# Loading and folding K's weight in halves of columns, decay vectors first, one output row in two halves: a gated mix of a state-space layer and linear attention

## The chip, the cores and the metric

The kernel runs on one core of a Trainium2 chip. A core has a matrix engine (PE, with its weight loads shown apart as PEld), a vector engine (DVE), a scalar engine (ACT), a general engine (POOL) and a queue engine that issues transfers (SP); ACT and POOL can issue transfers too. The metric is device time in microseconds, from the first to the last thing that the execution does. A profile is one execution with every instruction recorded; its "span" runs from the first to the last instruction, and the execution's own time is a little longer than that.

## The reference

The input x has 2048 rows of 512 values. Two branches read it, and a gate mixes them row by row:

```
g = sigmoid((x * gate_w).sum(-1))
out = g * A(x) + (1 - g) * B(x)
```

A is a diagonal state-space layer: x is projected to 512 complex states, each state runs the recurrence h = Lam_bar * h + Bu over the 2048 rows, with Lam_bar = exp(exp(log_dt) * (Lambda_re + i Lambda_im)), and the states are projected back; x * Dskip is added.

B is linear attention with 32 heads of 16 values. Q, K and V are x times three 512 x 512 blocks of wqkv. Q and K go through a small 16 x 16 matrix per head (w_phi), then through softmax of the result and of its negative, which gives 32 features per head; kv and z are sums over all rows of K's features (with V, and alone); each row's Q features read them, the quotient num / den is the head's output, and a 512 x 512 matrix wo ends the branch. All inputs and the output are bfloat16.

## The kernel before, in words

The rows are handled in 16 tiles of 128. x is loaded transposed, one tile by one DMA transpose from the SP queue (`x_load`, L228), into xT. w_phi is the same for all rows, so it is folded into the weights of Q and K once: a block-diagonal matrix BD is built from w_phi (`st_B`, L343, on DVE, with a mask that comes from an identity matrix made on POOL), K's weight is transposed on PE (`st_W`, L271), multiplied with BD (`fold`, L428, called by `st_f`), and copied to SBUF as Wk2. A K tile is then four matmuls of 512 columns (`st_k`, L477, through `tile_mm`), copied to Xq by `evac` (L117), on ACT or on DVE. Q's weight goes the same way later (`st_w`), V needs no fold (`st_v`).

K's features: DVE takes maxima and minima over the 16 values of a head by trees (`feat_max`, `feat_min`; the lines L511, L521, L527), ACT takes the exponentials (`feat_exp`, L138), DVE sums them (`feat_sum`), ACT takes logarithm and exponential of the sums, DVE scales. PE accumulates K's features with V over all tiles (`st_a`, L578). Q's features are made the same way in four groups of four tiles (A, 1, 2, 3), and are then transposed by DMA from SP (phT, L563).

The state-space branch interleaves rows by 8: input projections (`st_g`, L601, which need BT, the transposed B matrices, loaded as Bn by L284 and transposed by DMA at L288), a scan on DVE (`st_z`), and steps `st_h` that fill in the seven rows between. Its decay factors are small vectors: Lambda_im, Lambda_re and log_dt are loaded from POOL's queue into vec_n (L251, after the identity matrices and an iota), transposed on PE (`st_V`, L310), copied to vec (L312), and then a chain of short instructions on DVE and ACT makes angles, sines and powers (`st_P`, `st_P2` to `st_P4`, `st_U`, `st_i`, `st_M`). ACT holds one table set at a time, Exp/Ln or Sin: L130 loads the first, the first Sin (L144) brings the second, and L130 in `st_L` brings back the first.

Output: for every tile, `st_y` accumulates the state-space part in PSUM, `st_o` makes the attention output and transposes it (by DMA from SP, L758, or on PE for the last four), `st_t` multiplies with wo into the same PSUM bank, scales the row tile by the gate (L769 on ACT or L771 on DVE) and stores it (L773, from SP or ACT).

The order of the work is written out by hand. Every step is a Python generator that yields after each instruction group; the string ORDER names, word by word, which step runs on next. `k0@2` starts step k0 with PSUM bank 2, a later `k0` runs its next group, `:D` puts a copy or a scaling on DVE and not on ACT, `:A` puts a store on ACT's queue and not on SP's, and `F:28` issues 28 matmuls of 128 columns on a constant tile ("spin", results unused). PE, DVE, ACT and SP execute their instructions in just this order; an instruction that waits holds up all behind it on its engine.

Of the kernel before, what the change touches and what calls it, by code (L numbers as in the profile page):

```python
# [23 lines left out]
ORDER = """
B F:28 l11 F:4 W1@0 W0@1 W2@2 W1:D f1@3 W3@4 f1 W0:D f0@5 f0 NR W2:D f2@6 W3:D f3@0 f3 f2:D V@1 V P P P P2 P2 P2 P2 P2
P4 U P3 P4 P4 i1 i2 U l12 i1 i2 U F:4 k0@2 k0 NI P2 P3 l10 i0 l9 k1@3 k1 x0 i1 i1 i0 i2 k3@4 l14 x0 k2@5 n0 U M i1 k2
V2@6 v3@1 i2 x0 i0 v0@7 i0:D i0 v2@0 x0 k3 l8 n0 l13 i3 x0 k5@2 k5 i3 k4@3 v0 R0 x1 k6@5 n0 n0 i3 i3:D x1 x1 i2 k4 n0
v1@4 i3 L V2 k7@2 k7 n1 n1 x1 n1 gw x1 n1 R1 v6@7 e0 e0 v1 k6:D v4@6 n1 x2 n2 v7@3 v7 k11@2 v6 s0 x2 s0 e1 n2 s0 v5@5
v5 s0 s0 R2 D k12@4 R3 k10@3 k9@7 v4 k8@5 n2 l15 s0 e1 k13@6 v2 s1 k10 k14@0 s0 k11 C1 Q2 k8 C4 g20@3 s1 x2 k13 a0@25
k14 a0 n2 s1 k12 g20 x2 g00@6 k9 g30@0 s1 s1 s1 x2 n2 s1 v3 g40@4 x3 g01@3 g10@7 n3 R5 g00 a1 a1 x3 g60@1 n3 e2 R4  # L30
g11@6 g10 x3 g01 n3 e2 x3 e2 e2 n3 g11 k15@3 g60 g10 g30 g40 x3 s2 n3 g70@1 k15 g11 s2 x4 s2 s2 n4 g30 Q1 Q3 x4 n4 e3
e3 x4 C5 n4 Q0 x4 g50@7 g50 g50 s2 g21@4 n4 g21 s2 s2 v8@3 e3 e3 s3 g70 g70 g70 z0 s3 z0 g31@6 g31 s3 z0 z0 v11@0
g41@7 a2 C6 a2 g41 z0 z0 v11 g61@4 a2 g61 C7 w0@1 w0 C3 w1@7 w1 g31 a2 w2@0 w2 w3@4 s3 s3 g51@1 g51 g51 z0 R7 z0 x4
g62@7 w3 z0 z0 g71@6 g71 g02@0 v8 n4 s3 J2 g71 g71 z1 g02 z1 h50@1 h50 J2 z1 e4 e4 q1@4 h10@3 g62 g12@6 h10 g22@0 q2@1
z1 z1 z1 g22 q2 s3 z1 z1 q1 e4 h60@3 h60 g12 g12 z1 q3@7 q0@0 q0 q3 g32@1 e4 xA C2 g42@4 g32 nA g32 s4 g42 v9@6 v9 z1
s4 C0 J0 J0 g52@0 g52 c4 g52 nA c4 xA c4 R6 g72@7 g72 J1 s4 nA g23@3 g43@1 g03@4 g63@6 g72 g72 z2 h51@0 J3 c5 a3 g23
z2 J1 v10@7 h11@3 nA a3 c2 c2 g03 xA z2 z2 z2 z2 c0 h51 h61@4 z2 z2 g13@0 v10 xA h11 g43 c3 g13 a3 a3 J3 c5 z2 s4
g33@7 g13 g33 c0 z2 s4 s4 g33 h32@1 c2 h32 xA g53@3 g63 h52@0 g53 g53 nA s4 h52 h42@7 h42 eA c5 eA v14@1 v14 g73@6 g73
g73 q5@3 g73 h61 h12@0 h12 v12@1 v15@7 z3 z3 c0 z3 v12 eA eA h21@4 z3 v13@6 h21 a4 z3 z3 sA v13 z3 z3 c3 q10@0 q10
q6@1 v15 sA c1 c1 q4@4 q4 q6 a4 a4 c3 a4 h20@6 h30@0 h30 c7 q8@7 q12@4 q8 Y Y sA z3 z3 h33@2 q5 sA sA c1 h62@1 h20  # L40
h02@0 h33 sA sA q7@7 h62 G h43@3 h53@6 h02 c7 h13@2 Y Y sA q7 y6@1 h13 h01@0 h53 q12 c7 sA sA c6 q14@5 q14 h23@7 h23
h22@4 h31@2 h00@6 c6 q13@5 h31 h41@7 h43 c6 h22 h40@3 h63@2 h00 h41 h63 h40 h03@6 h03 sA sA y3@4 y3 END X1 o0@7 N1 X1
q13 o0 o0@2 O o0 N1 X1 q9@6 q9 N1 o1@3 X1 o1 o1@5 q11@7 o0 N1 X1 N1 o3@2 o1 o3 q11 X2 o1 o1 h01 X2 N2 X2 o3@6 o3 N2 X2
N2 E1 E1 E1 o1 E1 o0 o0 X2 S1 S1 N2 y0@3 o2@5 y0 y0 o2 o2@2 y3 o2 o2 y1@7 y1 S1 o3 o3 o3 S1 G y2@0 N2 q15@6 q15 S1 S1
o2 y1 o2 t1 S1 S1 G G y9@5 y9 E2 E2 y4@2 y4 y2 N3 E2 E2 y5@6 y9 y5 t1 S1 S1 S1 S1 X3 t3 t3 y2 t2 t2 X3 N3 N3 S2 X3 S2
t0 o4@7 y5 o4 o4@4 o4 N3 o4 X3 S2 y4 t0 y13@0 S2 o4 o5@7 o5 o5@4 o5 o5 y6 o4 y6 o6@3 S2 o6 o6@7 o6 X3 o5 y7@4 y7 o5 S2
S2 o7@3 N3 y13 o6 t4 t0:A o6 o6 E3 E3 E3 S2 S2 y8@7 t4:D o7:D E3 S3 t5 S2 S2 S2 t5 y12@2 S3 S3 o7@3 o7 o7 o7 t6 t6
o8@6 o8 o8@3 o8 o7 y12 y8 S3 t1:A o8 o8 o9@1 o9 o9@6 o8 y11@3 y11 S3 S3 y10@1 o9 o9 o9 S3 S3 t4:A o11@6 y7 t7 y12 o9
o11 t7 o10@6 y8 t8 t8 y11 y13 o11@4 t9 S3 S3 S3 o10 o11 S3 o10@7 t9:D y15@6 y14@4 o11 o11 o10 o10 t8:A o12@7 o12 o12@5
o12:D y15 o10 o12 o12 o11 o13@7 o13 o13@5 o13 o13 t2 y14 y14 o10 o12@7 t7:A t5:A o12:D o14@5 o14:D t3:A y10 o15@7 t9:A  # L50
y10 o15 o15@5 o15:D o15 o13 t12 o15 o14@7 o14 o14 t12:D t12 t11 t11:D o15@5 o15 o13@7 t10 t6:A t11 y15 o13:D t10 t10
t15 t15 t15:A o14 o14@2 t13 o14:D t13 t13 t14 t14 t14:A
# [16 lines left out]
def kernel(  # L69
# [198 lines left out]
    live = {}  # L268
    MM = nc.tensor.matmul

    def st_W(j):  # L271
        pt = bank([P, KT, P], BF16, "ptw")
        for k in range(KT):
            nc.tensor.transpose(pt[:, k, :], wk_nat[:, j, k * P:(k + 1) * P], ident[:])
# [198 lines left out]
    def tile_mm(pt, ti, W):  # L473
        for kt in range(KT):
            MM(out=pt[:], lhsT=xT[:, kt, ti * P:(ti + 1) * P], rhs=W[:, kt, :], start=(kt == 0), stop=(kt == KT - 1))  # L475
# [285 lines left out]
    def st_t(n):  # L761
        ti = order[n]
        py, oT = live["py", n], live["oT", n]
        for g in range(HG):
            MM(out=py[:], lhsT=oT[:, g, :], rhs=Wo[:, g, :], start=False, stop=(g == HG - 1))  # L765
        yield
        ot = pools["op"][1].tile([P, D], BF16, name="ot", bufs=14)
        if sel["eng"] == "act":
            nc.scalar.mul(out=ot[:], in_=py[:], mul=G[:, ti:ti + 1])  # L769
# [78 lines left out]
```

## Time and profile before

| | |
|---|---|
| median of 3 runs | 157.01 us (156.79 to 157.65) |
| the profiled execution's own time | 156.63 us |
| its span | 154.6 us |
| PE busy | 147.7 us, 96% |
| DVE busy | 131.8 us, 85% |
| ACT busy | 129.4 us, 84% |
| POOL busy | 16.1 us, 10% |
| granted PE clock, mean | 1.000 |

Busy time of PE counts the whole of each matmul, whose ends overlap with the next one's start, so 96% busy does not say that it runs at its peak; starts of matmuls have to be read for that. For DVE and ACT, too, one instruction's end overlaps with the next one's start by some 0.1 us. "Idle before, releaser" names what ended an engine's wait. SP, and the queues of ACT and POOL, show only the issue of a transfer as an instruction; the landing is later and is given as "to landing" from the start of the issue.

### The profile page before, as it was taken

The numbers are of one execution on the slowest core, as the hardware profiler recorded it, in microseconds if no ns is written. First come the engines' busy times: TensorE is split into PE (matmuls) and PEld (weight loads), VectorE is DVE, ScalarE is ACT, GpSimd is POOL, SyncE is SP. The second block draws the span as 40 slices with busy tenths as digits, with TensorE's granted clock in tenths as the row PEclk, the third lists the DMA queues.
The fourth block names the chain that finished last, engine by engine and source line by source line (L and its number), as shares of the span: only waits on it lengthen the run. The fifth ranks groups of instructions, "written<-read, shape, count | busy, mean of one in ns | idle before, by whom it ended". The sixth has DMA issues, their size and how long they took to land.

```text
span 154.6 us, 3382 instructions
## 1 busy us (share of the span) xinstructions
PE 147.7 (96%) x1254; PEld 95.6 (62%) x1254; DVE 131.8 (85%) x303; ACT 129.4 (84%) x279; POOL 16.1 (10%) x43
## 2 busy tenths in 40 slices
PE   7999999999999999999999999999998999989990
PEld 7844444797789876888755767454454545545540
DVE  3789999999999999999999999999997966423730
ACT  3489999999999999999999996799497998465652
POOL 8239980000000000000000000000000000000000
PEclk9999999999999999999999999999999999999999
DMA  4785998465475849910000006943169689789742
GB/s 120 158 222 87 168 191 170 89 98 107 97 78 105 174 94 168 184 25 6 0 0 4 0 0 136 141 136 68 34 123 143 117 163 197 150 137 200 208 147 94
DMA packets 50848, 17.55 MB, mean 113 GB/s; under 512 B 44176, under 2 KB 50832, under 8 KB 50832
## 3 DMA queue, kind: packets, MB, share of 16 engines
q1 hardware_dynamic: 48544, 15.36, 53.2%
q10 hardware_dynamic: 2128, 1.97, 4.5%
q8 instruction: 10, 0.16, 0.4%
q14 instruction: 6, 0.05, 0.1%
q0 software_dynamic: 160, 0.01, 0.1%
HBM read 2.64 MB, written 2.10 MB: 31 GB/s over the span
## 4 chain that ended last, share of the span: by engine, by line
DVE 47%; PE 32%; DMA 8%; ACT 6%; issue 4%; DVEq 0%; SPq 0%
PE py L717 9%; DVE smk L511 6%; PE pk L475 6%; DMA oT<-on 5%; PE py L765 5%; PE pgq L601 4%; DMA phT<-EEq 3%; DVE Bn L672 3%; DVE EEk L548 3%; DVE w L641 3%; DVE HM L672 3%; DVE H L652 3%; PE spin L812 3%; DVE EEk L527 2%; DVE EEk L521 2%
## 5 line engine op out<-in xcount | busy, mean ns | idle before, releaser
L601 PE MATMUL pgq<-xT,BT 128*128 128x256 bf16 x256 | 31.2, 272 | 0.0
L475 PEld LDWEIGHTS <-xT 128*128 128x128 bf16 x192 | 18.3, 98 | 18.6 <-DMA xT<-in_A_x_dram 0.8
L601 PEld LDWEIGHTS <-BT 128*128 128x128 bf16 x256 | 24.7, 98 | 3.9
L138 ACT ACTIVATE EEk<-EEk 128x1024 bf16<-128x1024 bf16 x20 | 20.6, 1075 | 0.3 <-DVE EEk L527 0.3
L765 PE MATMUL py<-Wo,oT 128*128 128x512 bf16 x64 | 16.1, 379 | 0.9 <-DMA oT<-on 0.9
L119 ACT CAST uv<-pgq 128x512 bf16<-128x512 f32 x28 | 16.3, 604 | 0.3
L475 PE MATMUL pq<-Wq,xT 128*128 128x512 bf16 x64 | 15.8, 379 | 0.0
L475 PE MATMUL pv<-Wv,xT 128*128 128x512 bf16 x64 | 15.6, 379 | 0.0
L475 PE MATMUL pk<-Wk,xT 128*128 128x512 bf16 x64 | 15.0, 379 | 0.3 <-ACT EEk L138 0.3
L138 ACT ACTIVATE ld<-pn 128x16 f32<-128x16 f32 x32 | 6.2, 193 | 7.6 <-PE pn L736 7.4
L138 ACT ACTIVATE EEq<-EEq 128x1024 bf16<-128x1024 bf16 x12 | 11.8, 1061 | 0.3 <-DVE EEq L527 0.3
L590 ACT ACTIVATE phT<-X,dgB 128x512 bf16<-128x512 bf16 x16 | 11.5, 740 | 0.0
L769 ACT ACTIVATE ot<-py,G 128x512 bf16<-128x512 f32 x12 | 8.0, 684 | 3.5 <-PE py L765 3.3
L119 ACT CAST nu<-pn 128x256 bf16<-128x256 f32 x28 | 10.3, 381 | 0.0
L736 PEld LDWEIGHTS <-phT 128*128 128x128 bf16 x128 | 6.7, 98 | 5.3 <-DMA phT<-EEq 1.2
L765 PEld LDWEIGHTS <-oT 128*128 128x128 bf16 x64 | 5.6, 97 | 6.2 <-DMA oT<-on 1.2
L119 ACT CAST vx<-pv 128x512 bf16<-128x512 f32 x16 | 9.4, 600 | 0.0
L548 DVE TENSOR_TENSOR EEk<-EEk,rck 128x4096 bf16<-128x4096 bf16 (+1 forms) x5 | 9.3, 1859 | 0.0
L119 ACT CAST Xq<-pq 128x512 bf16<-128x512 f32 x16 | 9.1, 610 | 0.2
L736 PE MATMUL pn<-KVm,phT 128*128 128x68 bf16 x128 | 8.0, 194 | 0.8 <-DMA phT<-EEq 0.7
L119 ACT CAST Xq<-pk 128x512 bf16<-128x512 f32 x15 | 8.4, 618 | 0.4 <-PE pk L475 0.4
L511 DVE TENSOR_TENSOR smk<-smk 128x512 bf16<-128x512 bf16 (+4 forms) x18 | 8.6, 476 | 0.1
(177 smaller groups left out, 319.6 us busy)
## 6 DMA issues: line engine op xcount, KB each, us to landing
X<-HM SPq DMA_DIRECT2D x8, 256.0 KB, 4.0
out_dram<-ot ACTq DMA_DIRECT2D x11, 128.0 KB, 2.5
out_dram<-ot SPq DMA_DIRECT2D x5, 128.0 KB, 2.5
C2r<-in_B_wqkv_dram ACTq DMA_DIRECT2D x2, 256.0 KB, 3.3
Wv<-in_B_wqkv_dram SPq DMA_DIRECT2D x1, 512.0 KB, 4.0
Bn<-in_A_B_re_dram SPq DMA_DIRECT2D x1, 512.0 KB, 5.5
Bn<-in_A_B_im_dram SPq DMA_DIRECT2D x1, 512.0 KB, 6.7
Wo<-in_B_wo_dram SPq DMA_DIRECT2D x1, 512.0 KB, 4.6
```

The costliest lines, as they stand in the source:

```text
L119: nc.scalar.copy(out=out_ap, in_=in_ap)
L138: ins = nc.scalar.activation(**kw)
L475: MM(out=pt[:], lhsT=xT[:, kt, ti * P:(ti + 1) * P], rhs=W[:, kt, :], start=(kt == 0), stop=(kt == KT - 1))
L511: VT(out=dst, in0=cur[:, :, :, 0:n, :], in1=cur[:, :, :, n:2 * n, :], op=op)
L548: VT(out=E5, in0=E5, in1=rc.to_broadcast([P, L, 2 * NB, Dh, 4]), op=ALU.mult)
L590: nc.scalar.mul(out=t_, in_=x_, mul=c_)
L601: MM(out=pg[:, h, :], lhsT=BT[:, kt, 2 * j + h, :], rhs=xT[:, kt, r * NC:(r + 1) * NC], start=(h == 0 and kt == 0), stop=(r % 2 == 0 and k ...
L672: VT(out=dst, in0=ph[:], in1=uv[j][:, r], op=ALU.add)
L717: MM(out=py[:], lhsT=hs(r, t, slice(a * P, (a + 1) * P)), rhs=C2B[t], start=(t == 0), stop=False)
L736: MM(out=pn[:, 4 * m:4 * m + 4, :].rearrange("p h e -> p (h e)"), lhsT=ph[:, 4 * hf + m, :], rhs=KVm[:, 4 * hf + m, :], start=(m == 0), st ...
L765: MM(out=py[:], lhsT=oT[:, g, :], rhs=Wo[:, g, :], start=False, stop=(g == HG - 1))
L769: nc.scalar.mul(out=ot[:], in_=py[:], mul=G[:, ti:ti + 1])
```

## The change

- K's weight comes from memory in two halves of columns (each with all 512 rows, 256 columns, so runs of 512 bytes), and not in two halves of rows (runs of 1024 bytes). The transposes of `st_W` then take a column block each and write one contiguous block of WTk; two of the four copies stand on ACT (W1, W3), two on DVE (W0, W2), where all four stood on DVE.
- The four fold steps make a half of the columns for two row blocks each, so the first two (f0, f1) need only the first half of the weight. The first four K tiles are computed in two halves of columns, eight matmuls of 256 columns each; their copy to Xq stays whole.
- The three loads of vec_n move ahead of the identity matrices on POOL's queue. The two loads of vec_m stay after the iota.
- Step t15 scales its row tile in two halves of columns and stores the halves with two transfers, one from ACT's queue, one from SP's. It is the last tile by number; t13 and t14 still come after it in the order, whole.
- ORDER is written anew. The multiset of steps is the same but for the extra groups of k0 to k3 and t15, and the constant matmuls: 24 and 4, where 28, 4 and 4 stood. The second part of B's input matrix (NI, A_B_im) is now the first of the two loads of Bn and stands ahead of the eight later x tiles on SP; the other one (NR) stands behind four of them (tiles 11, 14, 13, 8) and ahead of tiles 12, 9 and 10; tile 15's load stands after two of the BT transposes. Engine changes beside W1 and W3: the copy of f1 on DVE and that of f2 on ACT (before: the other way round), k7 for k6 on DVE, the absolute value of i3 on ACT (before on DVE), the scalings of t5 and t7 on DVE and those of t9, t11 and t12 on ACT, a copy of o13 on ACT and one more of o15 on DVE. The order of nearly all else shifts by some places.

```
-B F:28 l11 F:4 W1@0 W0@1 W2@2 W1:D f1@3 W3@4 f1 W0:D f0@5 f0 NR W2:D f2@6 W3:D f3@0 f3 f2:D V@1 V P P P P2 P2 P2 P2 P2
-P4 U P3 P4 P4 i1 i2 U l12 i1 i2 U F:4 k0@2 k0 NI P2 P3 l10 i0 l9 k1@3 k1 x0 i1 i1 i0 i2 k3@4 l14 x0 k2@5 n0 U M i1 k2
...
+NI B F:24 W1@0 W0@1 W1 W3@2 W3 W0:D V@3 V W2@4 W2:D P f0@5 f0 P f1@6 P F:4 l11 f1:D f3@0 P2 f2@1 k1@3 U f3 P2 f2 P2
+P2 P4 k0@2 P4 P4 P2 V2@4 k2@7 k0 k0 P3 P3 l14 k3@5 k1 k2 i0 i2 V2 i0 k1 k3 U i1 l13 k2 i2 i1 i1 U n0 i0 x0 i2 i0:D l8
+v3@6 v0@0 i0 k4@1 n0 NR n0 x0 l12 i2 v3 n0 l9 k5@4 x0 x0 i3 v4@2 l10 R0 k6@3 i3 k7@7 i2 x0 R1 i1 v2@6 n0 k3 x1 n1 i1
...
+T_SPLIT = (15,)
+K_SPLIT = 4
...
-    for k0 in (0, 2):
-        nc.scalar.dma_start(out=wk_nat[:, k0:k0 + 2, :], in_=B_wqkv[k0 * P:(k0 + 2) * P, D:2 * D].rearrange("(k p) n -> p k n", p=P))
+    for t_, srcs in ((vec_n, (A_Lambda_im, A_Lambda_re, A_log_dt)),):
+        for n, src in enumerate(srcs):
+            nc.gpsimd.dma_start(out=t_[4 * n:4 * n + 4, :], in_=src.rearrange("(j p) -> j p", p=P))
+    HD = D // 2
+    for c in range(2):
+        nc.scalar.dma_start(out=wk_nat[:, :, c * HD:(c + 1) * HD],
+                            in_=B_wqkv[:, D + c * HD:D + (c + 1) * HD].rearrange("(k p) n -> p k n", p=P))
...
-    def st_W(j):
+    def st_W(k):
         pt = bank([P, KT, P], BF16, "ptw")
-        for k in range(KT):
-            nc.tensor.transpose(pt[:, k, :], wk_nat[:, j, k * P:(k + 1) * P], ident[:])
-        yield
-        evac(WTk[:, :, j * P:(j + 1) * P], pt[:])
+        for j in range(KT):
+            nc.tensor.transpose(pt[:, j, :], wk_nat[:, j, k * P:(k + 1) * P], ident[:])
+        yield
+        evac(WTk[:, k, :].rearrange("p (j d) -> p j d", j=KT), pt[:])
         yield
...
-    def st_f(d):
-        return fold(Wk2, WTk, d)
+    def st_f(n):
+        c, d0 = n // 2, n % 2 * 2
+        pf = bank([P, 2, HD], F32, "pf")
+        for k in range(2):
+            for d in range(2):
+                MM(out=pf[:, d, k * P:(k + 1) * P], lhsT=WTk[:, 2 * c + k, (d0 + d) * P:(d0 + d + 1) * P], rhs=BD[:, 2 * c + k, :], start=True, stop=True)
+        yield
+        evac(Wk2[:, d0:d0 + 2, c * HD:(c + 1) * HD].rearrange("p d (hh f hl) -> p d hh f hl", hh=4, f=Dh),
+             pf[:].rearrange("p d (hh hl f) -> p d hh f hl", hh=4, hl=4))
+        yield
...
-        tile_mm(pk, ti, Wk2)
-        yield
+        if ti < K_SPLIT:
+            for c in range(2):
+                for kt in range(KT):
+                    MM(out=pk[:, c * HD:(c + 1) * HD], lhsT=xT[:, kt, ti * P:(ti + 1) * P], rhs=Wk2[:, kt, c * HD:(c + 1) * HD],
+                       start=(c == 0 and kt == 0), stop=(kt == KT - 1), skip_group_check=True)
+                yield
+        else:
+            tile_mm(pk, ti, Wk2)
+            yield
...
+        if n in T_SPLIT:
+            cols = [slice(c * D // 2, (c + 1) * D // 2) for c in range(2)]
...
+            for c in cols:
+                if sel["eng"] == "act":
+                    nc.scalar.mul(out=ot[:, c], in_=py[:, c], mul=G[:, ti:ti + 1])
+                else:
+                    VS(out=ot[:, c], in0=py[:, c], scalar1=G[:, ti:ti + 1], scalar2=None, op0=ALU.mult)
+                yield
+            for c in cols:
+                sel["q"].dma_start(out=out_par[:, ti // 2, ti % 2, c], in_=ot[:, c])
+                yield
+            return
```

More of the change, by code (lines that the diff above doesn't have):

```diff
@@ L30 @@
[L30 to L49, printed above, removed]
@@ L50 @@
-o12:D y15 o10 o12 o12 o11 o13@7 o13 o13@5 o13 o13 t2 y14 y14 o10 o12@7 t7:A t5:A o12:D o14@5 o14:D t3:A y10 o15@7 t9:A
-y10 o15 o15@5 o15:D o15 o13 t12 o15 o14@7 o14 o14 t12:D t12 t11 t11:D o15@5 o15 o13@7 t10 t6:A t11 y15 o13:D t10 t10
-t15 t15 t15:A o14 o14@2 t13 o14:D t13 t13 t14 t14 t14:A
+NI B F:24 W1@0 W0@1 W1 W3@2 W3 W0:D V@3 V W2@4 W2:D P f0@5 f0 P f1@6 P F:4 l11 f1:D f3@0 P2 P2 f2@1 k1@3 U f3 P2 f2 P2
+P2 P4 k0@2 P4 P4 P2 V2@4 k2@7 k0 k0 P3 P3 l14 k3@5 k1 k2 i0 i2 V2 i0 k1 k3 U i1 l13 k2 i2 i1 i1 U n0 i0 x0 i2 i0:D l8
@@ new lines @@
+v3@6 v0@0 i0 k4@1 n0 NR n0 x0 l12 i2 v3 n0 l9 k5@4 x0 x0 i3 v4@2 l10 R0 k6@3 i3 k7@7 i2 x0 R1 i1 v2@6 n0 k3 x1 n1 i1
+x1 n1 x1 x1 k4 l15 R2 gw U i3 i3 v1@5 n1 n1 v7@1 x1 k7:D k5 n1 k6 x2 i3 n2 L e0 k11@4 x2 n2 R3 x2 e0 k11 v2 v0 s0 e1
+s0 s0 Q2 s0 s0 k14@3 k14 s0 k13@7 k13 e1 C2 M D s0 v1 s1 v6@4 n2 x2 Q1 v5@6 k12@0 s1 k12 k9@3 k9 k8@7 k8 k10@5 n2 v6
+v5 a0@03 a0 v4 s1 g20@7 x2 k10 C0 v7 s1 g20 s1 g40@4 g40 Q3 g00@6 n2 x3 s1 e2 e2 e2 k15@2 k15 g01@5 g01 g50@1 s1 a1 x3
+a1 g21@7 n3 g00 x3 e2 n3 n3 x3 n3 g60@4 g60 g10@2 g10 g21 x3 C4 C5 g30@5 n3 s2 s2 x4 g10 s2 x4 s2 e3 e3 g11@6 g11 R5
@@ new lines @@
+t4 y12@1 N3 o6 t0:A S2 E3 o6 o6 o7 o7@7 E3 t5 S2 S2 S2 S2 o7:D y8@7 t6 E3 y13 t5:D t4:D E3 S3 o7 t6 S2 o8@2 o8 o8@0 o8
+o8 y13 o7 y11@3 o7 S3 o9@2 o9 S3 o9@0 S3 t4:A o8 S3 S3 o9 y12 y12 y10@2 o8 o9 S3 t1:A o9 o9 t6:A S3 S3 S3 y8 y11 y11
+o11@0 o11 t7 t7:D S3 S3 o11@0 o11 o11 y8 t8 o10@0 t8 t8:A t9 o10 o10@5 t9 o10 o10 o11 y15@7 y14@0 o11 o12@4 o12 o12@5
+y15 o12:D o12 o12 o10 o10 t2:A o13@4 o13 o13@5 o13 t5:A o13 y14 y15 t3:A o14@4 o14 o12@5 o12:D y10 y10 o15@5 t9 o15:D
+o13 o15@4 o15 o15 t12 t12 o14@5 o15 o14:D o14 o14 t11 t11 t12 o13@4 t11 o13 t7:A o15@5 t10 t10 o14@1 o15:D t15 t15 t15
@@ L53 @@
+y14 t10 t15:A t15 t13 t13 t13 o14:D t14 t14 t14:A
 """
 H_VECTOR = tuple((r, j) for r in (1, 2, 4, 5, 6) for j in range(4))
+T_SPLIT = (15,)
+K_SPLIT = 4
 OT_PE = (12, 13, 14, 15)
@@ L248 @@
     nc.gpsimd.iota(iot[:], pattern=[[1, NC]], base=0, channel_multiplier=0, allow_small_or_imprecise_dtypes=True)
-    for t_, srcs in ((vec_n, (A_Lambda_im, A_Lambda_re, A_log_dt)), (vec_m, (A_Dskip, gate_w))):
-        for n, src in enumerate(srcs):
-            nc.gpsimd.dma_start(out=t_[4 * n:4 * n + 4, :], in_=src.rearrange("(j p) -> j p", p=P))
+    for n, src in enumerate((A_Dskip, gate_w)):
+        nc.gpsimd.dma_start(out=vec_m[4 * n:4 * n + 4, :], in_=src.rearrange("(j p) -> j p", p=P))
     M2 = stg.tile([P, 4], F32, name="M2", bufs=1)
@@ L763, in st_t @@
         py, oT = live["py", n], live["oT", n]
+        if n in T_SPLIT:
+            cols = [slice(c * D // 2, (c + 1) * D // 2) for c in range(2)]
+            for g in range(HG):
+                MM(out=py[:], lhsT=oT[:, g, :], rhs=Wo[:, g, :], start=False, stop=(g == HG - 1))
+            yield
+            ot = pools["op"][1].tile([P, D], BF16, name="ot", bufs=14)
+            for c in cols:
[8 more added lines that the diff above has]
+            return
         for g in range(HG):
```

18 lines of the change are left out of this document (15 added, 3 removed).

## The prediction

> **What bounds the kernel now.** I read the page's first part and its chain, then the busy time by stretch, then the order of time at both ends.
>
> ```profile
> span 154.6 us, 3382 instructions
> PE 147.7 (96%) x1254; PEld 95.6 (62%) x1254; DVE 131.8 (85%) x303; ACT 129.4 (84%) x279; POOL 16.1 (10%) x43
> DVE 47%; PE 32%; DMA 8%; ACT 6%; issue 4%; DVEq 0%; SPq 0%
> ```
>
> ```profile
> 10.00:20.00 10.00, 10.00 (x49) 4.43 (x47) 9.90 (x37) 9.77 (x22) 8.66 (x22) 1.00 0.82 146
> 80.00:90.00 10.00, 10.00 (x98) 6.18 (x97) 9.91 (x26) 9.83 (x18) 0.00 (x0) 1.00 0.01 2
> 130.00:140.00 10.00, 9.43 (x85) 5.36 (x84) 3.36 (x6) 5.32 (x20) 0.00 (x0) 1.00 0.87 157
> ```
>
> In each stretch (columns PE, PEld, DVE, ACT, POOL, clock, DMA, GB/s) up to 90 us PE, DVE and ACT are full together. From the starts of matmuls PE also runs at its rate: 512 columns every 0.216 us. Between its first real work (4.4) and its last start the larger gaps are 0.23 and 0.24 (fold steps), 0.48 (23.0), 0.28 (100.2), 0.90 (116.8), 0.74 (136.3) and 0.48 (146.4); from 24 to 100 there is none above 0.05. DVE, taking each kind's usual distance from start to start, idles 0.9 us in all from 8 to 118. So neither engine alone can be made to gain: the end moves if all three start sooner, or if work leaves DVE and a PE gap closes.
>
> ```profile
> 1.11 3.59 PE L812 MATMUL spin<-fillw 128*128 128x128 bf16 x32 [1.11 <-DVE fillw L157]
> 4.50 1.08 PE L274 MATMUL ptw<-ident,C2r 128*128 128x128 bf16 x12
> 7.46 3.62 PE L475 MATMUL pk<-Wk,xT 128*128 128x512 bf16 x16
> 7.95 0.17 DVE L337 TENSOR_TENSOR ssm_par<-vec,ssm_par 128x8 f32<-128x8 f32 x1 [0.43 <-ACT ssm_par L138]
> 9.13 1.28 ACT L144 ACT_TABLE_LOAD   x1
> 16.53 0.59 SPq L284 DMA_DIRECT2D Bn<-in_A_B_im_dram  x1
> 17.48 1.28 ACT L130 ACT_TABLE_LOAD   x1
> 19.25 2.01 ACT L138 ACTIVATE EEk<-EEk 128x1024 bf16<-128x1024 bf16 x2
> 21.29 0.69 DVE L511 TENSOR_TENSOR smk<-EEk 128x1024 bf16<-128x1024 bf16 x1
> 23.69 2.27 PEld L475 LDWEIGHTS <-xT 128*128 128x128 bf16 x12 [0.80 <-DMA xT<-in_A_x_dram]
> ```
>
> The front, in order of time: constant matmuls until the weight is there, K from 7.46, the decay chain on DVE from 7.95, Sin tables at 9.13, Exp tables at 17.48, the first exponentials, the first sum right behind them (21.29), and one wait of PE for an x tile.
>
> ```profile
> 113.06 4.83 DMA phT<-EEq
> 117.94 0.30 PE pn L736 x4
> ...
> 132.98 4.04 DMA oT<-on
> ...
> 151.04 0.69 ACT ot L769
> ```
>
> The chain's end: DVE's last product of query group 1 (111.77) releases a DMA transpose, PE waits 0.90 for it, later 0.74 for an oT; then PE, one scaling, one store.
>
> **The change part by part.** Sums are against the profiled execution, 156.63 (span 154.6 and 2.0 around it); the median is 0.38 above it.
>
> *Weight in column halves, fold, split K.* The first half lands 3.28 after its issue at 0.79 (4.07), the second at 4.67. Packets of 1024 bytes took 46 ns, those of 256 bytes 18; at 512 bytes I estimate 27 from these, so a half's 512 packets over 16 engines need 0.87 instead of 0.74: landing 4.2 and 4.9. The 24 constant matmuls end at 1.11 + 24 x 0.107 = 3.68. So transposes run from 4.25 (before 4.39), 0.43 a step. ACT copies W1 at 4.95, W3 at 5.6, in its idle time (its first copy was at 6.09, after 2.91 idle); DVE copies W0 until 5.77; f0 at 5.83, its copy 6.27 to 6.86; f1's copy on DVE ends at 7.2. K's first half starts at 6.95, its third matmul at 7.25 with 0.22 of work done: as if from 7.03, so **PE leads by 0.43**. [...]
>
> *Decay vectors first on POOL.* Their issues (0.78, 0.53, 0.52) push the identities from 1.46 and 1.70 to 3.3 and 3.5. The transposes need the first at 4.25: covered by 0.9. DVE's mask, two small steps and BD follow at 3.7 to 5.4 (BD before: 3.92 to 4.61), just ahead of the W0 copy; if that slips, f0 does, bounded by 0.7, the shift of BD; I take 0. log_dt lands at 2.10 + 3.20 = 5.3 (before 6.47), V stands behind three transposes, and the decay chain starts on DVE at 6.35, not 7.95: **1.6 sooner**. Of that 0.6 goes to f1's copy, which now stands inside the chain, 0.1 to V2's; vec_m (4.9 + 3.1 = 7.5) is there when PE reaches V2 (7.9).
>
> *ACT.* Last fold copy at 7.95, so the Sin tables load at 7.95 instead of 9.13. Between the two loads stand all four first K copies (before three, one lay ahead), one more later K copy (0.48) and one more absolute value (0.31): the second load comes at about 17.1, the first exponentials at 18.4, not 19.25, since one K copy that stood between is now ahead. The first sum on DVE follows at 20.45: **0.85 sooner**, at equal work done on DVE (19.5 us in both orders). The x trees wait for K copies at 10.5 and 14.3; there DVE would be idle 0.1 to 0.7, and this is why 1.6 becomes 0.85.
>
> *Engine moves.* W1, W3 (0.34 each) and i3's absolute value (0.2) leave DVE: up to the last product of query group 1 it has 0.7 less work in all, some of it already in the 0.85. ACT has 1.1 more, 0.96 of it in early idle time.
>
> *SP and Bn.* NI moves up to 12.5, NR to 18.5 (behind four x tiles at 1.31 each); its landing is not known there: 4.0 (Wv, same size, 6.6 to 10.5) to 6.7 (NI before), nearest 5.5 (NR before, one x tile ahead of it, as here), so 24.0. Tile 12 is issued behind it; tiles behind a Bn load landed 0.44 and 0.58 after it: 24.5 (22.9 to 25.7). PE gets to k12 at 7.03 + 16.5 + 0.18 (the V2 gap) = 23.7, and waits 0.8 where it waited 0.48: there its lead shrinks from 0.43 to about 0.1 (from +0.9 to -1.1 between the ends). R0 needs both Bn loads: 24.1, as before 24.21. Tile 15 is issued at 26.7, lands by 31.3 (4.6), k15 is due at 31: 0 to 0.4.
>
> *Middle and end.* PE is 0.1 to 0.5 ahead, DVE and ACT 0.85; where DVE waits for PE it loses some of it, but its order puts z0 to S1 0.4 to 0.9 us of work earlier than before, so I let 0.85 stand at group 1's last product. Then phT lands at 117.0, where PE arrives at 116.9: the 0.90 gap closes. After that PE's order has the same steps at the same work (t9 at 128.7 us of work in both), and I keep the gaps at 136 and 146.
>
> *t15.* Two scalings for 0.69: from 0.69 (proportional) to 1.38 (no saving); nearest is the cast of 256 columns, 0.37 against 0.60 for 512, so about 0.85. ACT idles 0.42 before t13 and 0.16 before t14, which wait for PE; at worst t14 starts 0.1 later. One more SP issue (0.34) ends before t13's at 150.9. So 0; t14's full scaling and store still end the kernel. t9, t11, t12 against t5, t7: one more 0.69 on ACT, in its 5.0 us idle from 130 to 140: 0.
>
> **Sum:** 156.63 - 0.85 = 155.8, **156.1** against the median.
>
> **The rivals.** (1) *Eaten by the wait for x.* PE leads by only 0.1 at 28 us; if DVE's order then waits for PE wherever it is ahead (x4 behind the accumulation, the h sums at 88 to 96), only PE's lead is left: 156.9. For it: no PE gap from 24 to 100 that could close. Against it: the 0.90 gap belongs to DVE's chain.
>
> (2) *Slower: NR lands 6.7 after its issue.* Then 25.2, tile 12 at 25.7, k12 starts 2.0 late and PE is 1.1 behind before; R0 goes at 25.2 and g20 waits until 28.9. PE has no gap to make it up, DVE waits with it: +1.0, 158.0. It decides from a landing of tile 12 at 24.6 on. For it: NI took 6.68 when x tiles stood ahead of it; against it: NR took 5.54, and Wv 3.95.
>
> (3) *The matrix engine stays at half its rate.* Matmuls of 128 columns start 0.107 apart until 5.0 us, then 0.056. Now PE idles from 3.68 to 4.25, and if the full rate came a stretch like the first (3.9 us) later, the fold's 16 matmuls and K's first would take double: about 0.8 on PE by 8.4, partly hidden by the wait for tile 12: +0.4, 157.4. [...] No row here shows a gap that early.
>
> **How the numbers follow.** Forecast 0.42, own range 155.3 to 156.7; rival 1 0.28; rival 2 0.18; rival 3 0.12. A measurement of this kernel tells about 0.5%, 0.8 us, from no change: faster is below 156.2, slower above 157.8. Forecast gives 0.35 faster, 0.07 same; rival 1 0.04 faster, 0.22 same, 0.02 slower; rival 2 0.16 slower, 0.02 same; rival 3 0.02 faster, 0.05 same, 0.05 slower. Faster 0.41, same 0.36, slower 0.23. The range runs from the forecast's 155.3 to rival 2's 158.1.
>
> **What would show it.** Right: K's first matmul near 7.0, the decay chain near 6.4, Sin tables near 8.0, first exponentials near 18.4, no wait before o4 near 117. Wrong: starts 0.107 apart after 5.0 us; PE waiting over 0.9 for an x tile near 24, or for BT at 28; new PE gaps behind ACT's copies between 40 and 100, where the uv copies left it 0.14 to 0.4; a gap longer than 0.74 before t9.

## The result and the profile after

| | before | after |
|---|---|---|
| median of the executions | 156.82 us (20, from 156.09 to 158.1) | 158.26 us (20, from 156.84 to 159.9) |
| ratio to before, 95% interval | | 1.0065 (1.0036 to 1.0094) |
| profiled execution, its span | 156.63, 154.6 | 157.03, 155.2 |

The change makes the kernel slower by 0.65%, where 0.6% faster was forecast (156.1 us, range 155.3 to 158.1). The executions of the changed kernel fall apart into two groups: of the 15 that the ratio rests on, 6 took 156.84 to 157.34 and 9 took 157.76 to 158.77. The other five, 159.24 to 159.90, are classed as slow and left out of it; the medians in the table, which have them, differ by 0.9%. The profiled execution is of the lower group, so its trace shows only a part of the loss.

The profile page of the changed kernel, first part and chain, and two of its stretches (columns: PE, PEld, DVE, ACT, POOL, granted clock, DMA share, GB/s):

```profile
span 155.2 us, 3400 instructions
PE 147.2 (95%) x1262; PEld 96.6 (62%) x1262; DVE 131.4 (85%) x299; ACT 131.7 (85%) x284; POOL 14.0 (9%) x43
...
DVE 62%; PE 23%; DMA 6%; issue 4%; ACT 2%; POOL 1%; DVEq 0%; SPq 0%; POOLq 0%
```

```profile
10.00:20.00 10.00, 10.00 (x61) 5.72 (x61) 9.60 (x34) 9.75 (x23) 7.03 (x22) 1.00 1.11 167
80.00:90.00 10.00, 10.00 (x100) 6.32 (x99) 9.86 (x24) 9.89 (x18) 0.00 (x0) 1.00 0.01 2
130.00:140.00 10.00, 10.00 (x86) 5.54 (x85) 5.30 (x11) 5.45 (x22) 0.00 (x0) 1.00 1.11 181
```

The middle is as full as before. The differences are at both ends. PE's order of time at the front of the changed kernel (start, length, what; in brackets the idle time before it and what ended it):

```profile
4.08 1.52 PE L280 MATMUL ptw<-ident,C2r 128*128 128x128 bf16 x12 [0.23 <-DMA C2r<-in_B_wqkv_dram]
6.67 0.16 PE L316 MATMUL pvt<-ident,vec_n 12*128 12x12 bf16 x1 [1.07 <-DMA vec_n<-in_A_log_dt_dram]
6.77 0.40 PE L280 MATMUL ptw<-ident,C2r 128*128 128x128 bf16 x4
7.00 0.61 PE L447 MATMUL pf<-BD,Xq 128*128 128x128 bf16 x8
...
8.14 0.74 PE L496 MATMUL pk<-Wk,xT 128*128 128x256 bf16 x5
9.93 0.49 PE L496 MATMUL pk<-Wk,xT 128*128 128x256 bf16 x3 [1.05 <-ACT Wk L121]
```

V, the transpose of the decay vectors, now stands ahead of W2 and of all folds on PE and waits 1.07 us for log_dt. K's first half starts at 8.14 (before, K's first: 7.46), and behind five of its matmuls PE waits another 1.05 for a copy on ACT. The order of time of ACT, and of DVE where the first sum stands, gives the other half of that second wait, and what it does further on:

```profile
8.81 1.07 ACT L121 CAST Wk<-pf 128x512 bf16<-128x512 f32 x2 [0.69 <-PE pk L496]
9.90 1.28 ACT L146 ACT_TABLE_LOAD   x1
...
19.66 1.28 ACT L132 ACT_TABLE_LOAD   x1
20.95 2.00 ACT L140 ACTIVATE EEk<-EEk 128x1024 bf16<-128x1024 bf16 x2
```

```profile
23.05 0.68 DVE L532 TENSOR_TENSOR smk<-EEk 128x1024 bf16<-128x1024 bf16 x1
```

ACT's copies of the second half of the folded weight wait for PE's reads of the first half, though the two share no data. (Below, this is called the false wait.) So the Sin table comes at 9.90 (before 9.13; each of ACT's table loads takes 1.28), the first exponentials at 20.95 (19.25), the first sum at 23.05 (21.29). Late in the kernel the chain runs through the first transpose of query group 1:

```profile
113.07 1.19 DVE EEq L580
114.31 4.97 DMA phT<-EEq
```

DVE is 1.25 us later there (issue 114.31, before 113.06), 0.5 of the 1.76 having been made good. In both traces matmuls of 512 columns start 0.216 us apart where PE does not wait. How much later than at this rate PE's matmuls start, summed over a stretch: 5.03 us in the first ten (before 2.67), 0.13 from 20 to 30 (before 0.74; the wait of 0.48 for tile 12 is gone), 0.70 from 100 to 110 (0.36), 1.70 from 110 to 150 (2.75). Over the whole kernel this makes +1.1 us; eight constant matmuls fewer, at 0.054 by the same rate, take off 0.4; the span is 0.6 longer.

### The profile page after: what moved, and what is told of

Its sections match the earlier page's. It is cut to its first block, busy times and chain, and to the rows that moved or that the text cites. A ratio compares the mean times of both kernels' runs of the same rounds, so it can differ in the third digit from the quotient of the medians.

```text
span 155.2 us, 3400 instructions
## 1 busy us (share of the span) xinstructions
PE 147.2 (95%) x1262; PEld 96.6 (62%) x1262; DVE 131.4 (85%) x299; ACT 131.7 (85%) x284; POOL 14.0 (9%) x43
## 4 chain that ended last, share of the span: by engine, by line
DVE 62%; PE 23%; DMA 6%; issue 4%; ACT 2%; POOL 1%; DVEq 0%; SPq 0%; POOLq 0%
PE py L738 9%; DVE smk L532 8%; PE py L802 6%; DVE EEk L569 6%; DVE mxk L532 5%; DVE mnk L532 5%; DVE EEk L542 4%; DMA phT<-EEq 3%; DVE HM L693 3%; DVE Bn L693 3%; DVE H L673 3%; DMA vec_n<-in_A_log_dt_dram 3%; DVE w L662 2%; DVE EEk L548 2%; PE pn L757 2%
## 5 line engine op out<-in xcount | busy, mean ns | idle before, releaser
L622 PE MATMUL pgq<-xT,BT 128*128 128x256 bf16 x256 | 31.7, 272 | 0.0
L489 PEld LDWEIGHTS <-xT 128*128 128x128 bf16 x176 | 17.0, 98 | 16.4
L140 ACT ACTIVATE EEk<-EEk 128x1024 bf16<-128x1024 bf16 x20 | 21.1, 1106 | 0.0
L802 PE MATMUL py<-Wo,oT 128*128 128x512 bf16 x60 | 14.9, 379 | 0.0
L489 PE MATMUL pk<-Wk,xT 128*128 128x512 bf16 x48 | 11.2, 379 | 0.0
L121 ACT CAST Xq<-pq 128x512 bf16<-128x512 f32 x16 | 9.6, 625 | 1.1 <-PE pq L489 0.9
L532 DVE TENSOR_TENSOR smk<-smk 128x512 bf16<-128x512 bf16 (+4 forms) x18 | 8.1, 449 | 0.2
```

The costliest lines, as they stand in the source:

```text
L140: ins = nc.scalar.activation(**kw)
L532: VT(out=dst, in0=cur[:, :, :, 0:n, :], in1=cur[:, :, :, n:2 * n, :], op=op)
L622: MM(out=pg[:, h, :], lhsT=BT[:, kt, 2 * j + h, :], rhs=xT[:, kt, r * NC:(r + 1) * NC], start=(h == 0 and kt == 0), stop=(r % 2 == 0 and k ...
```

## Experiments

The first theory, A: the loss is made by the two stalls at the front. Its rivals: B, the front has slack and ACT's added work or the new order further on costs; C, the matrix engine's rate or the landing of Bn. Ratios are to the kernel before, run on the same chip beside each group of kernels.

### Undoing the two stalls, and the early vectors

Halves of Wk2 one behind the other (the later K tiles, not split, read both halves through a rearranged view):

```
+    Wk2h = Wk2[:].rearrange("p k d -> p (k d)").rearrange("p (c k n) -> p c k n", c=2, k=KT)
-        evac(Wk2[:, d0:d0 + 2, c * HD:(c + 1) * HD].rearrange(...
+        evac(Wk2h[:, c, d0:d0 + 2, :].rearrange(...
-                    ... rhs=Wk2[:, kt, c * HD:(c + 1) * HD],
+                    ... rhs=Wk2h[:, c, kt, :],
```

> Wk2 is laid out with its two column halves one behind the other (each half's 4 x 256 values contiguous), nothing else changed. Theory A (the loss is made at the front, by two stalls of PE; the second, 1.22 us at 8.6, is a wait between halves that share no data but lie interleaved in one tile): the copy of f3 on ACT no longer waits for k1's first half (8.81 becomes about 8.1), k0's first half follows k1's without the 1.05 wait, the Sin table load goes from 9.90 to about 8.9, the first sum from 23.05 to about 22.1, and the time falls to 0.998 to 1.002 of before (changed kernel: 1.0065). Rival B (PE's front has slack; what costs is ACT's 1.1 us of added work, or the new order further on): the wait goes, the time stays at 1.005 to 1.008. Rival C (the matrix engine's rate or the landing of Bn sets it): as B, and 0.107 between starts after 5 us, or a wait before k12 that takes the gain.

V behind f1:

```
-... W0:D V@3 V W2@4 W2:D P f0@5 f0 P f1@6 P F:4 l11 f1:D ...
+... W0:D W2@4 W2:D f0@5 f0 f1@6 V@3 V P P P F:4 l11 f1:D ...
```

> The transpose of vec_n (V) moves on PE from ahead of W2, f0 and f1 to behind f1's matmuls, its copy on DVE behind W2's; nothing else changed. Theory A: the 1.07 wait for vec_n's landing (6.67) is then filled with W2, f0 and f1; f0 goes from 7.00 to about 6.1, k1's first half from 8.14 to about 7.6; the second stall stays and swallows part of it, so the time is 1.001 to 1.005 of before. Rival B: 1.005 to 1.008. A third reading (the chain of decay vectors, not K, carries the delay): DVE's first product of the chain stays at 7.5 and the first sum within 0.2 of 23.05, time 1.005 to 1.008 too.

Both at once:

> Both of the above: the halves contiguous, and V behind f1. Theory A: both stalls gone, K's first half at about 7.5 and no wait over 0.5 behind it, first exponentials at about 19.3 (before 19.25, changed 20.95), time 0.993 to 0.999 of before. Rival B: 1.005 to 1.008. Rival C: the wait for tile 12 near 24 us comes back with 0.5 to 1.0 and the time stays above 1.000.

The loop that loads vec_n, moved back to just ahead of vec_m's:

> The three loads of vec_n go back behind the identity matrices and the iota on POOL's queue, as in the kernel before; all else as changed. The prediction's step was that moving them first makes the decay vectors land 1.2 sooner. In the changed kernel log_dt landed at 6.54 (before 6.47), so the theory now says: they land at 6.3 to 6.7 here as well, the identities are there by 2.0 and not by 4.1, the first stall stays, time 1.004 to 1.008 of before. If the move did gain something that the one profile does not show, log_dt lands at 7 or later here and the time is over 1.010.

| | median, us | ratio (95%) | V on PE | K's first | first sum |
|---|---|---|---|---|---|
| contiguous halves | 158.31 | 1.0084 (1.0060 to 1.0107) | 6.76 | 9.39 | 24.63 |
| V behind f1 | 156.62 | 0.9989 (0.9966 to 1.0012) | 6.73 | 7.50 | 22.84 |
| both | 157.46 | 1.0023 (0.9999 to 1.0046) | 7.92 | 9.29 | 23.66 |
| vectors back | 161.54 | 1.0226 (1.0174 to 1.0279) | 7.06 | 9.69 | 27.17 |

Theory A explains neither. V behind f1 brought K's first to 7.50 as expected, and the time even below the 1.001 to 1.005 that A had said. But its first sum is only 0.21 earlier than the changed kernel's (22.84 against 23.05), and DVE keeps about this lead up to 120 us; there it grows to 0.65, where a block of PE's code came at 115.09 and not at 117.34 (see the part on PE's code). Most of the rest of the way from 1.0065 to 0.9989 is that the changed kernel's times stand mostly in its upper group; its lower one, near 157.0, would give 1.001. So by these profiles V's own price is about 0.2 us. With the halves the theory failed outright (0.998 to 1.002 expected). The contiguous layout did remove the false wait: ACT's copies now wait for the fold and not for K. (Order of time of ACT, contiguous halves.)

```profile
9.21 1.07 ACT L121 CAST Wk<-pf 128x512 bf16<-128x512 f32 x2 [0.59 <-PE pf L448]
10.30 1.28 ACT L146 ACT_TABLE_LOAD   x1
```

But everything was later, and the reason stands in PE's own rate: with contiguous halves, with both, and with the vectors back, matmuls of 128 columns still started 0.107 us apart at 7 us, and the rate doubled only at 12.9, 9.8, and past 16 us; in the changed kernel's own profile it doubled (to 0.056 apart, below called the full rate) by 5.2, with V behind f1 by 4.5. With the vectors back in their old place log_dt lands at 6.93, not 6.54. Whether the early place is worth these 0.4 us is not shown, since in the kernel before, with the same place and the same issue times, it landed at 6.47. And 0.4 us is not that kernel's 1.6%, for it also has the low rate longest.

### The rate

A new theory, D: in the upper group the full rate comes late, because PE now idles for 0.49 (3.5 us), 0.35 (4.8) and 1.23 (5.4), in the time in which the rate doubles in the lower group. Filling the stretches with constant matmuls starts nothing sooner:

```
-NI B F:24 W1@0 W0@1 W1 W3@2 W3 W0:D V@3 V ...
+NI B F:27 W1@0 W0@1 W1 F:4 W3@2 W3 W0:D F:11 V@3 V ...
```

> The changed kernel with constant matmuls put into the idle stretches of PE's front and nothing else: 27 in place of 24 ahead of W1, 4 ahead of W3, 11 ahead of V. Theory D (new, from the runs before: the matrix engine's rate decides; in three of the four kernels it stood at 0.107 between starts of 128 columns until 9.8, 12.9 and past 16 us, and the changed kernel's own executions fall into a group near 157.0 and one from 157.8 to 159.9): with no gap over 0.2 ahead of 6.6, the full rate comes at about 5 us in every execution, the group near 158.8 is gone, median 156.7 to 157.3, ratio 1.000 to 1.004. Theory A (only the stalls themselves count): nothing that waits starts sooner, so 1.006 to 1.009 as in the changed kernel.

The same with V behind f1 (27, 4, and 6 ahead of f0), and with the contiguous halves as well:

> V behind f1 as tried before (0.9989), with constant matmuls in the gaps that are left: 27 ahead of W1, 4 ahead of W3, 6 ahead of f0. Theory D: full rate at about 5 us in all executions, the highest times (157.9) go; ratio 0.994 to 0.998. Theory A: 0.998 to 1.000, and a little worse if the constant matmuls delay f0.

> The halves of Wk2 contiguous, V behind f1, and the constant matmuls as in the kernel beside it. The two kernels with contiguous halves ran their folds at the low rate (0.107), so what the contiguous halves bring could not be seen. Theory D with the false wait as a second cost: full rate at about 5, no wait of 1.05 at 8.4, K's first at 7.5, Sin tables near 9.0, first exponentials near 19.7, ratio 0.985 to 0.995. If the false wait costs nothing (K's copies on ACT are what counts): as V behind f1 with constant matmuls, 0.994 to 0.999. Theory A alone would have put the kernel without constant matmuls (1.0023) below 0.999.

And a gap in the kernel before:

```
-B F:28 l11 F:4 W1@0 ...
+B F:12 l11 W1@0 ...
```

> The kernel before, with 12 constant matmuls ahead of the weight's transposes in place of 28 + 4: PE idles from 2.4 to 4.1, and the transposes can start at 4.1, 0.4 sooner than before. Nothing else is touched. Theory D: the full rate then comes at 7.5 us or later in most executions, K's first matmul at 7.8 or later, and the time is 1.004 to 1.015 of before with a wide spread. Theory A and rival B (the rate is no cause): a gap in front of the first real matmul is free, 0.997 to 1.001.

| | median, us | ratio (95%) | full rate from | first sum |
|---|---|---|---|---|
| filled (42) | 156.54 | 0.9976 (0.9954 to 0.9997) | 5.7 | 23.07 |
| filled, V behind f1 | 156.34 | 0.9972 (0.9952 to 0.9991) | 4.5 | 23.05 |
| the same, contiguous halves | 155.97 | 0.9942 (0.9917 to 0.9967) | 4.2 | 22.38 |
| before, with a gap | 156.81 | 0.9991 (0.9971 to 1.0012) | 8.9 | 22.33 |

One of the twelve executions of the filled kernel stands apart (158.16), the rest are 155.75 to 157.02. Filling gained more than D had said: 0.9976, where the lower group of the changed kernel, at 157.0, would give 1.001. And the gap in the kernel before did delay the rate, to 8.9 us, and the first sum by 1.04, but its time did not move: D missed there. Two things are seen in its trace. Half of the delay is made good on the way: the first transpose of query group 1 is issued at 113.62, 0.56 later than before. And that kernel has 20 constant matmuls fewer, which, as the next part shows, changes how long that transpose takes: it landed after 3.24 us and not 4.83. So this run does not tell what the late rate alone costs there.

With the rate held, the false wait can be priced: contiguous halves bring 0.2 to 0.3% (156.34 to 155.97, 0.9972 to 0.9942). The intervals overlap, so the time alone does not settle it; the traces do say that the first sum comes 0.67 earlier and the first transpose of query group 1 is issued 0.95 earlier (113.28 against 114.23). PE's wait of 1.05 for ACT's copy is gone; the other wait, 0.30 for DVE's copy, stays. (PE's order of time, the kernel filled, with V behind f1 and contiguous halves.)

```profile
7.49 0.38 PE L497 MATMUL pk<-Wk,xT 128*128 128x256 bf16 x2
8.18 0.81 PE L497 MATMUL pk<-Wk,xT 128*128 128x256 bf16 x6 [0.31 <-DVE Wk L123]
```

### Why filling gained too much: PE's code

Instruction by instruction, DVE of the filled kernel stands within 0.1 us of the changed kernel's profile up to 120 us, and there it is 0.92 ahead. The step is made by the first transpose of query group 1, which landed 3.26 us after its issue and not 4.97. The trace has one more user of the transfer engines: code, on a queue of its own (q8, "instruction": 10 packets, 0.16 MB in the changed kernel, so blocks of 16 KB), ten in an execution, nine in the kernel before with a gap; in the changed kernel each block took 0.88 to 1.53 us. It is PE's: from one block to the next PE goes on by 247 to 268 instructions, weight loads counted (changed kernel), and DVE by anything from 20 to 53. One came at 117.34 in the changed kernel, among these transposes; 18 constant matmuls more, each with its weight load, brought it at 111.13. The view of transfers from 113 to 121 us, in 40 slices, of the changed kernel:

```profile
DMA  0000008992003999998699990000007999999999
GB/s 0 0 0 0 0 8 179 214 210 45 0 0 68 218 223 204 205 193 169 119 200 287 122 24 0 0 8 9 10 10 156 288 275 292 291 289 288 273 285 260
...
q8 instruction: 1, 0.02, 0.7%
```

The block (queue q8) took from 117.34 to 118.22; from 117.8 to 119.0, for 1.2 us, the transposes all but stand still (0 to 10 GB/s). So theory E: the filled kernel gained by the shift of its code. Four kernels separate D from E. (`FW:n` stands for n constant matmuls of 512 columns, `S:n` for n small ones, of 32 columns in the third kernel and of 72 in the fourth.) The changed kernel again, on the chip of the others:

> The changed kernel as it is, on the chip of the three beside it. Theory D (two levels: full rate at about 5 us, or not before 9): median 157.8 to 158.8, single times from 156.8 to 159.9, ratio 1.004 to 1.010; if the profiled execution is of the upper group, its starts stand 0.107 apart past 7 us. Theory E (new: what e_fill gained is not the rate, but that PE's code, fetched in blocks of 16 KB by the same transfer engines, no longer falls among query group 1's transposes: block at 111.13 and not at 117.34, transposes landing 3.26 after their issue and not 4.97) says the same of this kernel.

Filled, with the changed kernel's number of instructions:

```
-NI B F:24 W1@0 W0@1 W1 W3@2 W3 W0:D V@3 V ...
+NI B F:15 FW:3 W1@0 W0@1 W1 FW:1 W3@2 W3 W0:D FW:2 F:3 V@3 V ...
```

> The same idle stretches of PE's front are filled as in the kernel with 42 constant matmuls, for as long, but with 24 instructions as in the changed kernel (six of them 512 columns wide), so that PE's code blocks stay where they were. Theory D: the upper group of times goes, median 156.8 to 157.4, ratio 0.999 to 1.003; a block at about 117 with a transpose of group 1 landing 4.5 to 5.0 after its issue. Theory E alone: 1.005 to 1.009, as the changed kernel beside it.

Only more instructions:

```
-... f2 P2 P2 P4 k0@2 ...
+... f2 P2 P2 P4 S:18 k0@2 ...
```

> The other half: 18 more instructions on PE, as in the kernel with 42, but as matmuls of 32 columns in the wait at 8.6 us, so that the early gaps stay and only the code blocks shift. Theory E: the block that stood at 117.34 comes at 111 to 112, transposes of group 1 land 3.2 to 3.5 after their issue, no gap over 0.3 near 118, the lower group of times moves to 155.9 to 156.4; with theory D beside it the upper group stays at 157 to 159, median 157.0 to 157.8, ratio 1.000 to 1.005. Theory E alone: 0.996 to 0.999 with a spread under 1.5 us. Theory D alone: 1.005 to 1.009.

More instructions in the kernel before:

```
-B F:28 l11 F:4 W1@0 ...
+B S:52 l11 S:6 W1@0 ...
```

> The kernel before, with its 32 constant matmuls of 128 columns ahead of the weight made into 58 of 72 columns: the same time on PE, 52 instructions more, so PE's code block of 115.65 comes some 4 us sooner, ahead of query group 1's transposes (first issue 113.06, landing 4.83). Theory E: landing about 3.3, the 0.90 gap of PE at 116.8 closes to under 0.3, ratio 0.994 to 0.998. If the block and the slow landing have nothing to do with each other: landing 4.4 to 4.9 and ratio 0.999 to 1.002.

| | median, us (all) | ratio (95%) | PE's code block | first phT of group 1, us to landing |
|---|---|---|---|---|
| changed, again | 158.76 (158.47 to 159.1) | 1.0127 (1.0098 to 1.0157) | 118.96 | 5.03 |
| filled, same count | 157.35 (157.01 to 157.57) | 1.0042 (1.0022 to 1.0062) | 117.24 | 5.04 |
| count only | 156.37 (155.87 to 158.16) | 1.0000 (0.9970 to 1.0031) | 111.25 | 3.26 |
| before, more instructions | 156.33 (155.51 to 157.24) | 0.9978 (0.9956 to 0.9999) | 109.83 | 3.23 |

Both hold, each for its part: the filled kernel of unchanged count lies at 1.0042, between what D said (to 1.003) and what E alone said (from 1.005), and the count alone brought the lower group to 155.87 to 156.69. This time the changed kernel was profiled in its upper group. PE's order of time there, and the fold's instructions by their form (duration in ns: lowest, median, highest):

```profile
6.65 0.16 PE L316 MATMUL pvt<-ident,vec_n 12*128 12x12 bf16 x1 [1.14 <-DMA vec_n<-in_A_log_dt_dram]
...
7.14 1.06 PE L447 MATMUL pf<-BD,Xq 128*128 128x128 bf16 x8
...
9.28 1.27 PE L496 MATMUL pk<-Wk,xT 128*128 128x256 bf16 x5
11.50 0.49 PE L496 MATMUL pk<-Wk,xT 128*128 128x256 bf16 x3 [0.95 <-ACT Wk L121]
```

```profile
L447 PEld LDWEIGHTS <-Xq x16: 151/151/151, 7.0 to 9.1; 128*128 128x128 bf16 x16
L447 PE MATMUL pf<-BD,Xq x16: 314/314/314, 7.1 to 9.2; 128*128 128x128 bf16 x16
```

The same fold in the kernel filled at the same count:

```profile
L447 PEld LDWEIGHTS <-Xq x16: 95/98/98, 6.9 to 8.0; 128*128 128x128 bf16 x16
L447 PE MATMUL pf<-BD,Xq x16: 219/219/229, 6.9 to 8.0; 128*128 128x128 bf16 x16
```

V starts at 6.65 and 6.59, and so is not the difference. K's first comes at 9.28 and at 8.06, the first sum at 24.60 and 22.96, the median is 1.4 us apart, and the code block comes at the same distance behind the first transpose's issue (3.09 and 3.10): that is the rate alone. The traces show it for one execution of each group; the others are put into the groups by their times.

The code alone is the other row pair. Transfers from 113 to 121 us, count only, where no code block falls:

```profile
GB/s 0 0 0 0 0 23 206 221 184 21 0 0 102 221 216 209 205 186 159 138 212 211 200 216 202 137 159 218 207 214 206 183 132 168 215 220 200 218 197 82
```

In DVE's order count only and the changed kernel's first profile stand within 0.1 us up to 120 us, and there the former is 1.02 ahead: that is the block alone. Landing times of phT in that stretch, first the kernel before, then the kernel before with more instructions:

```profile
DMA to landing us min/median/max: 3.1/4.4/4.8
```

```profile
DMA to landing us min/median/max: 3.1/3.3/3.3
```

All seventeen profiles of this study fit: in the eleven where the block came 1.0 to 3.1 us after the first transpose's issue, that transpose took 4.55 to 5.04 us; in the five where it came 1.8 to 3.8 us ahead of the issue, 3.23 to 3.28; and in the kernel before with a gap, whose block came 6.0 us behind it (119.63), the first two took 3.24 and 3.26 and the next two 5.23 and 4.73. The kernel before gains 0.2% by its shift, the low end of what E said; but the shift also costs there. Its first block came at 8.95 and not 12.33, amid the front's loads: Wv, issued at 6.58 in both, landed at 12.12 and not 10.53, PE stood idle for 0.9 until it was there (11.3 to 12.2), and the first sum came 1.04 later. So its price is not that of the late block alone.

### Which stretch, and the split of t15

```
-NI B F:24 W1@0 W0@1 W1 W3@2 ...
+NI B F:18 FW:2 W1@0 W0@1 W1 F:4 W3@2 ...
```

> The changed kernel, its 24 constant matmuls made as long as 26 (two are 512 columns wide) and moved in part: the idle stretches at 3.5 and 4.8 us are filled, V's wait at 5.4 is not; the number of instructions on PE is unchanged. If the first two stretches decide (the rate opens by about 5.2 and a later gap does not close it): no upper group, median 156.9 to 157.5, ratio 1.001 to 1.005. If V's wait decides: as the changed kernel, median 158.0 to 158.9, 1.007 to 1.013.

```
-NI B F:24 W1@0 W0@1 W1 W3@2 W3 W0:D V@3 V ...
+NI B F:20 FW:1 W1@0 W0@1 W1 W3@2 W3 W0:D FW:3 V@3 V ...
```

> The opposite: only V's wait is filled (three matmuls of 512 columns ahead of it), the stretches at 3.5 and 4.8 stay; again the same number of instructions. If the first two stretches decide: in part of the executions the rate still comes late, at about 7 to 9 us, median 157.5 to 158.7, with both groups. If V's wait decides: one group, 156.9 to 157.5.

On top of the kernel filled at the same count, `T_SPLIT = ()` and two words `t15` less:

> All three stretches filled at an unchanged count (1.0042 there), and step t15 scaled and stored whole, as in the kernel before. The prediction priced the split at nothing: then 1.003 to 1.006. If the second scaling and the second store delay the last two rows, 1.000 to 1.003; if the split helps, over 1.006.

The first gave 157.26 us, ratio 1.0050 (1.0020 to 1.0079), with ten executions at 156.99 to 157.56 and two at 158.47 and 159.12; its profile is one of these two, with the rate doubling between 10.1 and 11.4. The second gave 157.26, 1.0036 (1.0008 to 1.0064), eleven at 156.99 to 157.58 and one at 159.2. So neither stretch alone decides: with either filled, executions like the upper group are rarer (2 and 1 of 12) than in the changed kernel. With all three filled there were none of 11, but the filled kernel of 42 had one of 12 (158.16), and so has the one with t15 whole (158.14); that all three are better than one is not shown. t15 whole: 157.30, 1.0042 (1.0021 to 1.0064), just as with the split (1.0042): no cost and no gain that could be measured.

## Why the prediction was wrong

The term of the sum that failed is "the first sum 0.85 sooner": it was 1.76 later where the full rate came early, and 3.3 later (24.60) where it did not. Three steps lead there: the decay vectors that did not land sooner, with V in front of the folds; the halves that did not overlap; and the half rate, which the sum left out, as a rival with a chance of 0.12.

**Decay vectors: "log_dt lands at 2.10 + 3.20 = 5.3", "1.6 sooner".** Wrong. The loads' issues began at 1.32, not at 0.79, and log_dt took 3.93 us from issue to landing and not 3.20, a row measured on an issue at 3.27. It landed at 6.54, against 6.47 before. The first packet of these loads moved at 4.25, and at 4.30 in the kernel before, though their first issue came 0.65 sooner: an earlier issue did not bring an earlier transfer. What holds them until then is open.

**"V stands behind three transposes."** So it does, but it also stands ahead of W2 and of every fold, and no price was put on its being late. PE waited 1.07 for it, and K's first half came at 8.14 and not 6.95. With V behind f1, K's came at 7.50, but the first sum only 0.21 sooner.

**The split halves overlap: "K's first half starts at 6.95", with the second half copied beside it.** Copies and reads of the halves were ordered against each other where they lay interleaved in one tile (ACT waited 0.69 for PE, then PE 1.05 for ACT; with contiguous halves ACT waited for the fold); that wait was not seen. ACT's copies were not done at 7.95 but at 9.88, so the tables went to 9.90 and 19.66, and the first sum to 23.05 in place of 20.45. With the rate held, the wait is worth 0.67 at the first sum, and 0.2 to 0.3% of the time.

**Rival 3, the half rate.** This decided the median. The half rate was named, with the early gap as its cause; filling the gaps made it rare, though not all runs agree (below). But the chance (0.12) and the size (+0.4, 157.4) were wrong: 9 of 15 executions, then all 5 of a second set, and 1.4 us. The prediction saw one gap, from 3.68 to 4.25; there were three, because the second half of the weight landed at 5.16 and not 4.9 (0.35) and V waited (1.23). And it took the price on PE alone, where ACT's tables and DVE's first sum move with it by 1.6. The point of the doubling varies from execution to execution: one and the same kernel doubled its rate by 5.2 us in one and between 10.1 and 11.5 in another. The late rate cost 0.9% between the kernels of like code (1.4 of 157) and 1.3% between the two profiles of the changed kernel (159.10 and 157.03).

**"First sum 0.85 sooner" carried to the end, "the 0.90 gap closes".** The first sum was 1.76 later, but the last product of group 1 only 1.25; delay at the first sum is not all delay at group 1, as the kernel before with a gap shows too (1.04 later there, 0.56 here). The 0.90 gap (0.55 after) was put down to DVE's chain. Most of it was the stop of the transposes for PE's code: with the block moved, PE's wait for phT in the kernel before fell from 0.73 to 0.2 though DVE was later (issue 113.64 against 113.06).

**Right:** NR (forecast to land at 24.0) landed at 23.72, tile 12 (24.5) at 24.19, and rival 2 did not come; PE, itself late, no longer waited for x near 24 at all. t15's two scalings took 0.84 (estimated 0.85), at no cost. The identities, though they ended at 4.1 and not at 3.5, came with the first half of the weight (4.04); only BD, ending at 5.7, was later than the 5.4 of the working. The range, which ended at rival 2's 158.1, missed the median by 0.2.

What remains: with the rate held and the code where it was, the changed kernel is at 1.004, and its first sum at 22.96, 1.67 later than before: that is the part of V and the false wait, and of whatever else delays the front. Why the count-only kernel, whose front has the same three stretches, had only 3 of 12 executions at 157.7 to 158.2 is not settled; whether its 18 small matmuls at 8.75 us have a part in it was not tried. So that the gaps make the rate late is likely and not fully shown, and what sets the point of the doubling in an execution was not tried.

The best version of these, filled, V behind f1 and contiguous halves, beats both kernels: 155.97 us, 0.9942. It has both of the change's ideas, without its two long waits, and its code block falls at 111.5. That the ideas themselves bring anything is not shown: its first sum is still 1.09 later than in the kernel before, and the first transpose of group 1 is issued 0.22 later (113.28 against 113.06). It gets ahead only where that transpose lands, after 3.28 us and not 4.83.

## What to carry to other kernels

Price an early gap on the matrix engine by what the half rate does to every engine behind it, and not by the gap, and fill it with constant matmuls: here the late rate cost 1.4 us, and with all three gaps filled 2 of 35 executions stood apart (158.14 and 158.16), where the changed kernel had 9 of 15 and 5 of 5 in its upper group. A step moved forward on an engine's order needs its data's landing looked up on that side too (V: a wait of 1.07), and halves that should overlap are worth a contiguous layout: interleaved, they were ordered here as if they shared data (1.05). Before crediting an experiment's gain, compare instruction by instruction where it appears: here the gain of 18 extra matmuls in the first 7 us appeared at 118.

## What was not expected of the hardware

- The granted clock does not show the half rate: it is 1.00 from 4 to 8 us in both groups, while 128 columns take 219 or 314 ns and a weight load 98 or 151. (First the changed kernel in its upper group, then its first profile.)

```profile
4.00:8.00 4.00, 2.85 (x26) 2.48 (x27) 2.50 (x10) 1.56 (x4) 1.39 (x4) 1.00 0.81 152
```

```profile
4.00:8.00 4.00, 2.75 (x35) 2.31 (x36) 2.80 (x11) 1.95 (x5) 1.39 (x4) 1.00 0.78 156
```

- PE's code arrived in blocks of 16 KB during the run (q8: 10 packets, 0.16 MB), and a block amid the DMA transposes of group 1 held these up: 4.55 to 5.04 us to landing in place of 3.23 to 3.28. Thirteen to 26 matmuls more on PE, placed in the first 9 us, moved it by 5 to 6 us.
